# A fused attention, expert and gated-product kernel: first loads in three parts, a shorter mask set-up, out-weights ahead of block weights, two last tiles moved up

## The chip, the cores and the metric

The kernel runs on one core of one Trainium2 chip. Its time is the device time of one execution in microseconds (us); 590.64 us is the median of three runs (589.14 to 592.86). The engines are PE (TensorE matmul, with its weight loads as PEld), DVE (VectorE), ACT (ScalarE), POOL (GpSimd) and SP (SyncE, which here issues DMAs). Each engine executes its own list of instructions in order and waits on semaphores for the others.

## The reference

Three stages run one after the other in fp32.

1. Attention for 2 batches, 8 heads, 768 positions, head size 64, with a local window of `n_local` = 96 keys, `n_global` = 8 keys seen by all, and a bias that grows with distance at a slope of its own for each head:

```python
keep = is_global | is_local
dist = np.where(is_global & ~is_local, float(n_local), np.abs(rel))
slopes = 2.0 ** (-8.0 * (np.arange(H) + 1) / H)
scores = np.where(keep, scale * q @ k.T - slopes * dist, -1e9)
a = softmax(scores); out = a @ v
```

2. Each of the 1536 tokens (512 wide) goes to one of 8 experts: relu(x @ w1[e]) @ w2[e], times two gate factors.
3. (x @ w_a * (x @ w_b)) @ w_out with 1536 inner columns.

## The kernel before

Instructions stand in the order in which they are written; no scheduler moves them. What order each engine has comes from the order of the Python statements.

**Attention** (about 0 to 90 us). There are 24 units of two query tiles by two heads: `units` runs over batch, head pair `p` and `m` = 0, 1, 2. A loop over `n` (line 760 on) runs the steps of different units side by side: `score(n)` (PE scores, DVE adds the bias table and takes the row extremum, ACT the exponential), `trans(n-1)` (PE transposes, DVE and ACT copy), `rows(n-3)`, `av(n-2)`. The keys are laid out so that each query tile sees one stretch of key columns. A table `bias[h]` of 128x384 for each head holds slope times distance plus -1e30 where a key is masked; `dist` and `mk` are built once on DVE, and `make_bias(h)` makes a table on DVE: two ahead of the loop, six within it. Keys and queries of a head pair are loaded by `loadk` and `loadq` from SP's queue into pools of three buffers each; those of pair 0 come in two parts (key columns 0 to 288 and queries 0 to 256 for m = 0; the rest for m = 1 and 2). SP issues in order, and a load into a used buffer waits until its readers are done. `flags()` tests the two integers on DVE, and `nbad` reads the outcome into a register of every engine.

**Router and experts** (about 87 to 300 us). Weights are loaded, split into a high and a low fp32r part (`split_to`) on ACT, DVE and POOL, and used by PE.

**The gated product** (about 300 us to the end) runs in steps f = 0 to 11, one for each 128 inner columns; from f = 2 on `seven(f)` is the step. It forms the products of three groups of 512 tokens (`c` = 0, 1, 2), two of them by seven half-products over sums of blocks. Tiles of the output, `out_tile(p, c, t)`, are made for pairs of steps p = f // 2: `both(p)` puts twelve on a list at the end of an odd step, and `fill(n)` takes n of them off. A tile is six matmuls into a bank `ps_o` (lines 1312 to 1314: gh by wh, gh by wl, gl by wh for both steps of the pair); in the last pair each is added to `acc` on DVE (line 1319) and written by an indirect DMA that POOL issues (line 1321).

Weights of this stage come as int64 words. `conv1` (ACT), `conv2` (DVE, POOL) and `conv3` turn half a weight block into fp32r: `conv3` casts `wh` on ACT (line 1027) and takes the remainder `wl` on POOL (line 1028). Each step prepares the two halves of the next step's block weights (`jobs`) and half of an out-weight block: its `conv3` is put on the list `late` in one step and executed in the next. So the second half for pair p is finished in odd step f = 2p + 1, at whose end the first tiles of the pair read it. In the last step no block weights follow.

Of the kernel before, what the change touches and what calls it, by code (L numbers as in the profile page):

```python
# [12 lines left out]
F32 = mybir.dt.float32  # L13
# [34 lines left out]
def moe_block_kernel(ctx, tc, qd, kd, vd, kt, vn, nv, wg, wg2, we, wm, out):  # L48
# [467 lines left out]
    with ExitStack() as att:  # L516
# [27 lines left out]
        K0, K1, Q0 = 288, 192, 256  # L544
        loadk(0, 0, K0)
        loadq(0, 0, Q0)
        loadk(0, K1)
        loadq(0, Q0)
# [4 lines left out]
        make_identity(nc, ident)  # L553
        G.tensor_copy(idg[:, :, 0:P], bc(ident.unsqueeze(1), [P, 4, P]))

# [5 lines left out]
        t1 = bia.tile([P, P], F32, name="t1")  # L561
        t2 = bia.tile([P, P], F32, name="t2")
        iota(rel[:, 0:128], [[-1, 128]], base=96, cm=1)
        iota(rel[:, 128:256], [[-1, 128]], cm=1)
        iota(rel[:, 256:384], [[-1, 128]], cm=1)
        iota(kid, [[1, 128]])
        G.tensor_scalar(t1, rel[:, 128:256], 0.0, None, ALU.is_ge)
        G.tensor_copy(dist[:, 0:256], rel[:, 0:256])
# [6 lines left out]
        V.tensor_scalar(mk[:, 0:128], rel[:, 0:128], nl_f, None, ALU.is_lt)  # L575
        V.scalar_tensor_tensor(mk[:, 128:256], rel[:, 128:256], nl_f, t1, ALU.is_lt, ALU.mult)
        V.tensor_scalar(t2, kid, ng_f, None, ALU.is_lt)

        V.scalar_tensor_tensor(dist[:, 256:384], rel[:, 256:384], nl_f, mk[:, 128:256], ALU.subtract, ALU.mult)
        V.tensor_tensor(mk[:, 256:384], mk[:, 128:256], t2, ALU.max)  # L580
        V.tensor_scalar(dist[:, 256:384], dist[:, 256:384], nl_f, None, ALU.add)

        V.tensor_copy(mk[:, 96:128], t2[:, 0:32])
        V.tensor_scalar(dist[:, 96:128], rel[:, 96:128], 0.0, nl_f, ALU.mult, ALU.add)
        V.tensor_scalar(mk, mk, BIG, -BIG, ALU.mult, ALU.add)
        bias = [bia.tile([P, 384], F32, name=f"bias{h}") for h in range(H)]

        def make_bias(h):
            V.scalar_tensor_tensor(bias[h], dist, -8.0 * 2.0 ** -(h + 1), mk, ALU.mult, ALU.add)

        make_bias(0)
        make_bias(1)
# [10 lines left out]
        def score(u):  # L603
# [7 lines left out]
            ko, qo = (0, 0) if bp or m == 0 else (K1, Q0)  # L611
# [153 lines left out]
        for n in range(nu + 3):  # L765
            for f in RS.get(n, ()):
                f()
            if n < nu:
                b, p, m = units[n]
                nxt = b * 4 + p + 1  # L770
                if m == 1 and nxt + 1 < 8:
                    loadk(nxt + 1)
                    loadq(nxt + 1)
                if m == 2 and nxt < 8:
                    for j in range(2):
                        loadv(2 * nxt + j)
                if b == 0 and p < 3 and m:
                    make_bias(2 * p + 1 + m)
                score(units[n])
# [15 lines left out]
            if n == 1:  # L795
                flags()
            if n == 3:
                nbad = nc.values_load(ctl_i[0:1, 17:18], min_val=0, max_val=1, skip_runtime_bounds_check_because="a flag")
# [535 lines left out]

    def c2(*js):
        conv2(*js)
        for _ in js:
            cload(nc.sync)


    def seven(f):
# [32 lines left out]
        V.tensor_tensor(v, pc, p1, ALU.add)  # L1374
        if f % 2:
            ab2(0)
        else:
            fill(4)
# [3 lines left out]
        if f % 2:  # L1382
            ab2(1)
            low[2]()
        for j in jobs:
            conv3(j)
        while late:
            f_, j = late.pop(0)
            f_(j)
# [12 lines left out]
        low[0] = gate(0, f, pa)  # L1402
        mul(pb, T4, A22, False, True, True)
# [3 lines left out]
        low[0]()  # L1407
        low[1]()
        if f % 2:
            both(f // 2)  # L1410
            fill(3)
            rest()
            fill(3 if f < 11 else 9)
        else:
            ab2(0)
            rest()
            ab2(1)
            low[2]()
# [106 lines left out]
```

## Time and profile before

| | us |
|---|---|
| runs: median (lowest to highest) | 590.64 (589.14 to 592.86) |
| profiled execution: its own time | 590.52 |
| its span, first to last instruction | 588.5 |
| PE busy | 562.5 (96% of the span) |
| DVE busy | 412.8 (70%) |
| ACT busy | 307.7 (52%) |
| POOL busy | 266.1 (45%) |

The span is the time from the first to the last instruction of the profiled execution; 2.0 us of its own time lie outside it. Busy time counts an instruction from its start to its end, so PE is called busy also where its matmuls overlap: the matmuls of the last stage last 0.39 us each and start 0.23 us apart.

### The profile page before, as it was taken

The page shows a single profiled execution, that of the slowest core. Times are in us where ns is not written, and L with a number is a line of the kernel's source. Part 1 is how long each engine was busy: PE and PEld are TensorE (multiplying, and loading weights), DVE is VectorE, ACT ScalarE, POOL GpSimd, SP SyncE. Part 2 cuts the span into 40 slices and gives each one's busy share as a digit, 9 for nine tenths or more (in the row PEclk, how much of TensorE's full clock was granted, in tenths as well). Part 3 has the DMA queues.
Part 4 walks back from the last instruction along what each step waited for, and adds up shares of the span by engine and source line. Part 5 has one row for each costly group of instructions (what it writes and reads, how often), then busy time and mean ns, then how long its engine had stood idle before and what let it go on. Part 6 is the DMA issues. An engine that isn't in the chain of part 4 may idle for free. (4 is left out here: it accounts for less than half of the span.)

```text
span 588.5 us, 10238 instructions
## 1 busy us (share of the span) xinstructions
PE 562.5 (96%) x3476; PEld 485.2 (82%) x3476; DVE 412.8 (70%) x985; ACT 307.7 (52%) x710; POOL 266.1 (45%) x259
## 2 busy tenths in 40 slices
PE   5999999989999998999999999999899999999995
PEld 4787777978999998999978788788788878878884
DVE  6889986636945788776856777676676686686563
ACT  4877784457655766767564665505414423442210
POOL 3344580655515364545343336425624534344235
PEclk9999999999999998999999999999999999999998
DMA  8676772348576777788661021230120302200014
GB/s 279 241 248 222 308 196 104 109 155 287 169 237 234 230 253 273 229 261 275 225 205 42 33 82 63 72 108 36 73 80 28 108 36 73 107 36 1 2 42 174
DMA packets 39264, 87.30 MB, mean 148 GB/s; under 512 B 6001, under 2 KB 17009, under 8 KB 39201
## 3 DMA queue, kind: packets, MB, share of 16 engines
q1 hardware_dynamic: 32256, 74.25, 37.5%
q0 software_dynamic: 2192, 6.95, 3.3%
q10 hardware_dynamic: 4752, 5.34, 2.9%
q8 instruction: 31, 0.51, 0.4%
q14 instruction: 33, 0.26, 0.1%
HBM read 73.28 MB, written 13.23 MB: 147 GB/s over the span
## 5 line engine op out<-in xcount | busy, mean ns | idle before, releaser
L127 POOL TENSOR_TENSOR wl<-st,wh 128x512 fp32r<-128x512 f32 x58 | 75.2, 1317 | 73.2 <-ACT wh L123 61.3
L1016 POOL TENSOR_TENSOR tx<-tx,st 128x512 int32<-128x512 int32 x36 | 52.4, 1467 | 96.7 <-DVE tx L1014 42.3
L479 PE MATMUL ps_y<-h,wl 128*128 128x224 f32 (+7 forms) x288 | 74.7, 259 | 0.0
L123 ACT CAST wh<-st 128x1024 fp32r<-128x1024 f32 x56 | 59.1, 1056 | 28.9 <-DMA st<-we 28.0
L475 PE MATMUL ps_y<-h,wh 128*128 128x448 f32 (+5 forms) x224 | 68.3, 370 | 4.4 <-DVE h L497 3.2
L127 DVE TENSOR_TENSOR wl<-st,wh 128x1024 fp32r<-128x1024 f32 x35 | 49.0, 1399 | 28.7 <-ACT wh L123 28.6
L479 PE MATMUL ps_h<-x,wl 128*128 128x224 f32 (+6 forms) x256 | 66.9, 261 | 0.0
L1028 POOL TENSOR_TENSOR wl<-tx,wh 128x512 fp32r<-128x512 f32 x36 | 48.6, 1374 | 24.3 <-ACT wh L1027 24.3
L1313 PE MATMUL ps_o<-wl,gh 128*128 128x512 f32 x144 | 56.5, 393 | 3.0 <-POOL wl L1028 3.0
L627 ACT ACTIVATE pe<-pe,mx 128x256 f32<-128x256 f32 (+1 forms) x96 | 45.9, 479 | 22.6 <-DVE mx L623 22.6
L1319 DVE TENSOR_TENSOR acc<-ps_o,acc 128x512 f32<-128x512 f32 x60 | 40.8, 689 | 23.6 <-PE ps_o L1314 23.5
L1312 PE MATMUL ps_o<-wh,gh 128*128 128x512 f32 x144 | 56.2, 390 | 0.9 <-ACT acc L1317 0.9
L475 PE MATMUL ps_h<-x,wh 128*128 128x448 f32 (+4 forms) x192 | 56.3, 363 | 0.5 <-DVE yt L507 0.3
L1314 PE MATMUL ps_o<-wh,gl 128*128 128x512 f32 x144 | 56.1, 389 | 0.0
L479 PEld LDWEIGHTS ps_y<-h,wl 128*128 128x128 f32 x288 | 55.8, 194 | 0.0
L475 PEld LDWEIGHTS ps_y<-h,wh 128*128 128x128 f32 x224 | 42.9, 191 | 8.3 <-ACT hs L495 3.0
L479 PEld LDWEIGHTS ps_h<-x,wl 128*128 128x128 f32 x256 | 48.8, 191 | 0.0
L1267 POOL TENSOR_TENSOR wl<-tt,wh 128x512 fp32r<-128x512 f32 x20 | 25.5, 1300 | 49.1 <-ACT wh L1265 49.1
L623 DVE CUSTOM_DVE_ANT_0 pe<-ps_s,bias 128x256 f32<-128x256 f32 (+1 forms) x96 | 32.8, 398 | 7.8 <-PE ps_s L617 6.9
L475 PEld LDWEIGHTS ps_h<-x,wh 128*128 128x128 f32 x192 | 36.1, 188 | 2.0 <-DVE yt L507 0.5
L1265 ACT CAST wh<-tt 128x1024 fp32r<-128x1024 f32 x10 | 10.5, 1052 | 49.4 <-DVE tt L1260 49.4
L1313 PEld LDWEIGHTS ps_o<-wl,gh 128*128 128x128 f32 x144 | 27.0, 188 | 10.1 <-POOL wl L1028 4.6
(341 smaller groups left out, 1508.1 us busy)
## 6 DMA issues: line engine op xcount, KB each, us to landing
st<-we SPq DMA_DIRECT2D x64, 512.0 KB, 4.6
st<-wm SPq DMA_DIRECT2D x32, 512.0 KB, 3.5
vc<-vd SPq DMA_DIRECT2D x16, 352.0 KB, 5.2
k<-kd SPq DMA_DIRECT2D x7, 464.0 KB, 6.0
y_dram<-zero SPq DMA_DIRECT2D x12, 256.0 KB, 6.5
x_dram<-x SPq DMA_DIRECT2D x6, 512.0 KB, 3.2
acc<-y_dram SPq DMA_DIRECT2D x6, 512.0 KB, 5.0
q<-qd SPq DMA_DIRECT2D x7, 384.0 KB, 6.2
```

Source lines behind the costliest of these rows:

```text
L123: A.copy(wh, st)
L127: eng.tensor_tensor(wl[:, r], st[:, r], wh[:, r].bitcast(F32), ALU.subtract)
L475: T.matmul(pt[:, 0:2 * n].rearrange("p (s n) -> p s n", s=2), a, M[:, k], start=(k == 0), stop=False)
L479: T.matmul(pt[:, 0:n], b, M[:, k, 0], start=False, stop=(k == last))
L623: V.tensor_tensor_reduce(out=pe[:, t_, j, 0:n], in0=ps[:, j, t_, 0:n], in1=bias[2 * p + j][:, b0:b0 + n], op0=ALU.add, op1=ALU.min, scale= ...
L627: A.activation(pe[:, t_, j, 0:n], pe[:, t_, j, 0:n], AF.Exp, bias=mx[:, t_, j:j + 1], scale=-1.0, accum_out=sm[:, t_, j:j + 1])
L1016: lambda t=txi, l=l: G.tensor_tensor(t, t, l, ALU.add)))
L1028: G.tensor_tensor(wl_, tx, wh.bitcast(F32), ALU.subtract)
L1312: T.matmul(po, gh, wh, start=(i == 0), stop=False)
L1313: T.matmul(po, gh, wl, start=False, stop=False)
L1314: T.matmul(po, gl, wh, start=False, stop=(i == 1))
L1319: V.tensor_tensor(at, po, at, ALU.add)
```

## The change

There are five edits.

- The first keys and queries come in three parts, one for each `m` of pair 0 (`cuts`). All three buffers of both pools are then in use, and the loads of pair 1, which stand next but four in SP's list, wait for the readers of the first part.
- The mask set-up is written anew. POOL marks keys that lie ahead of the query by a distance of 1e6 (`FAR`) before DVE starts, and DVE then needs five operations for `mk` and `dist` instead of nine. Tables 0 and 1 are made on DVE, the second as half the first; tables 2 to 7 are made on POOL ahead of the loop as multiples of table 1. `make_identity` and the copy into `idg` come behind POOL's mask operations.
- `flags()` moves from n = 1 to n = 3 and the register loads `nbad` from n = 3 to n = 5.
- In `seven(f)` the list `late` (the out-weights) is worked off ahead of the block weights (`jobs`), and in step 11 as soon as `v` is formed.
- In step 11 two tiles of the last pair come ahead of the last six matmuls on `pb`, one between its DVE operations, and nine at the end.

```diff
--- before.py
+++ after.py
@@ -541,55 +541,45 @@
 
         nc.sync.dma_start(nv_i, nv.partition_broadcast(P))
 
-        K0, K1, Q0 = 288, 192, 256
-        loadk(0, 0, K0)
-        loadq(0, 0, Q0)
-        loadk(0, K1)
-        loadq(0, Q0)
+        cuts = [(0, 288, 0), (192, 608, 256), (512, KW, 512)]
+        for a, b, q0 in cuts:
+            loadk(0, a, b)
+            loadq(0, q0, q0 + 256)
         for bh in range(2):
             loadv(bh)
         nc.sync.dma_start(wg_sb, wg)
         nc.sync.dma_start(idg[:, :, P:P + 32], wg2)
-        make_identity(nc, ident)
-        G.tensor_copy(idg[:, :, 0:P], bc(ident.unsqueeze(1), [P, 4, P]))
-
 
         dist = bia.tile([P, 384], F32, name="dist")
         mk = bia.tile([P, 384], F32, name="mk")
         rel = bia.tile([P, 384], F32, name="rel")
         kid = bia.tile([P, P], F32, name="kid")
-        t1 = bia.tile([P, P], F32, name="t1")
-        t2 = bia.tile([P, P], F32, name="t2")
+        FAR = 1e6
+        own = rel[:, 128:384].rearrange("p (a n) -> p a n", a=2)
         iota(rel[:, 0:128], [[-1, 128]], base=96, cm=1)
-        iota(rel[:, 128:256], [[-1, 128]], cm=1)
-        iota(rel[:, 256:384], [[-1, 128]], cm=1)
+        iota(own, [[0, 2], [-1, 128]], cm=1)
+        G.affine_select(out=own, in_=own, compare_op=ALU.is_ge, fill=FAR, base=0, pattern=[[0, 2], [-1, 128]], channel_multiplier=1)
+        G.memset(rel[:, 96:128], FAR)
         iota(kid, [[1, 128]])
-        G.tensor_scalar(t1, rel[:, 128:256], 0.0, None, ALU.is_ge)
-        G.tensor_copy(dist[:, 0:256], rel[:, 0:256])
+        make_identity(nc, ident)
+        G.tensor_copy(idg[:, :, 0:P], bc(ident.unsqueeze(1), [P, 4, P]))
 
         V.tensor_copy(nv_f, nv_i)
         nvr = nv_f[:, :].rearrange("p (a b) -> p b a", b=2)
         V.scalar_tensor_tensor(nval, nvr[:, 0, :], 0.0, nvr[:, 1, :], ALU.is_lt, ALU.add)
         V.scalar_tensor_tensor(nval, nval, 4294967296.0, nvr[:, 0, :], ALU.mult, ALU.add)
 
-        V.tensor_scalar(mk[:, 0:128], rel[:, 0:128], nl_f, None, ALU.is_lt)
-        V.scalar_tensor_tensor(mk[:, 128:256], rel[:, 128:256], nl_f, t1, ALU.is_lt, ALU.mult)
-        V.tensor_scalar(t2, kid, ng_f, None, ALU.is_lt)
-
-        V.scalar_tensor_tensor(dist[:, 256:384], rel[:, 256:384], nl_f, mk[:, 128:256], ALU.subtract, ALU.mult)
-        V.tensor_tensor(mk[:, 256:384], mk[:, 128:256], t2, ALU.max)
-        V.tensor_scalar(dist[:, 256:384], dist[:, 256:384], nl_f, None, ALU.add)
-
-        V.tensor_copy(mk[:, 96:128], t2[:, 0:32])
-        V.tensor_scalar(dist[:, 96:128], rel[:, 96:128], 0.0, nl_f, ALU.mult, ALU.add)
-        V.tensor_scalar(mk, mk, BIG, -BIG, ALU.mult, ALU.add)
+        V.tensor_scalar(mk[:, 256:384], kid, ng_f, -BIG, ALU.is_ge, ALU.mult)
+        V.tensor_scalar(mk[:, 0:256], rel[:, 0:256], nl_f, -BIG, ALU.is_ge, ALU.mult)
+        V.tensor_scalar(dist, rel, nl_f, None, ALU.min)
+        V.tensor_copy(mk[:, 96:128], mk[:, 256:288])
+        V.tensor_tensor(mk[:, 256:384], mk[:, 128:256], mk[:, 256:384], ALU.max)
         bias = [bia.tile([P, 384], F32, name=f"bias{h}") for h in range(H)]
 
-        def make_bias(h):
-            V.scalar_tensor_tensor(bias[h], dist, -8.0 * 2.0 ** -(h + 1), mk, ALU.mult, ALU.add)
-
-        make_bias(0)
-        make_bias(1)
+        V.scalar_tensor_tensor(bias[0], dist, -4.0, mk, ALU.mult, ALU.add)
+        V.tensor_scalar(bias[1], bias[0], 0.5, None, ALU.mult)
+        for h in range(2, H):
+            G.tensor_scalar(bias[h], bias[1], 0.5 ** (h - 1), None, ALU.mult)
         xt = {}
 
         units = [(b, p, m) for b in range(B) for p in range(4) for m in range(QT // 2)]
@@ -608,7 +598,7 @@
             mx = wrk.tile([P, 2, 2], F32, tag="mx", bufs=3, name="mx")
             sm = wrk.tile([P, 2, 2], F32, tag="sm", bufs=5, name="sm")
             bp = b * 4 + p
-            ko, qo = (0, 0) if bp or m == 0 else (K1, Q0)
+            ko, _, qo = cuts[0 if bp else m]
             for t_ in range(2):
                 i = 2 * m + t_
                 k0, n, b0 = geom(i)
@@ -774,8 +764,6 @@
                 if m == 2 and nxt < 8:
                     for j in range(2):
                         loadv(2 * nxt + j)
-                if b == 0 and p < 3 and m:
-                    make_bias(2 * p + 1 + m)
                 score(units[n])
             if 0 <= n - 1 < nu:
                 trans(units[n - 1])
@@ -792,9 +780,9 @@
             for _ in range(4 if n >= 3 else 0):
                 if cl:
                     cl.pop(0)()
-            if n == 1:
+            if n == 3:
                 flags()
-            if n == 3:
+            if n == 5:
                 nbad = nc.values_load(ctl_i[0:1, 17:18], min_val=0, max_val=1, skip_runtime_bounds_check_because="a flag")
             if n in LD:
                 eload(0, LD.index(n))
@@ -1332,6 +1320,11 @@
 
     late = []
 
+    def lates():
+        while late:
+            f_, j = late.pop(0)
+            f_(j)
+
     def c2(*js):
         conv2(*js)
         for _ in js:
@@ -1372,6 +1365,8 @@
         V.tensor_tensor(u2, pb, p1, ALU.add)
         mul(pc, T1, S1, True)
         V.tensor_tensor(v, pc, p1, ALU.add)
+        if f == 11:
+            lates()
         if f % 2:
             ab2(0)
         else:
@@ -1382,11 +1377,9 @@
         if f % 2:
             ab2(1)
             low[2]()
+        lates()
         for j in jobs:
             conv3(j)
-        while late:
-            f_, j = late.pop(0)
-            f_(j)
         for j in wo:
             conv1(j)
         for _ in nxt:
@@ -1400,17 +1393,26 @@
         V.tensor_tensor(u2, pc, u2, ALU.add)
         V.tensor_tensor(pa, u2, pa, ALU.mult)
         low[0] = gate(0, f, pa)
+        if f == 11:
+            both(f // 2)
+            fill(2)
+            low[0]()
         mul(pb, T4, A22, False, True, True)
         V.tensor_tensor(pb, pb, p1, ALU.add)
         V.tensor_tensor(pb, pb, v, ALU.mult)
         low[1] = gate(1, f, pb)
-        low[0]()
+        if f == 11:
+            fill(1)
+        else:
+            low[0]()
         low[1]()
-        if f % 2:
+        if f == 11:
+            fill(9)
+        elif f % 2:
             both(f // 2)
             fill(3)
             rest()
-            fill(3 if f < 11 else 9)
+            fill(3)
         else:
             ab2(0)
             rest()
```

DVE's list from its third operation on, where mask and bias tables are made (`rel`, `kid`: distances and key numbers from POOL; `nval`: the two integers); before:

```order
L573 SCALAR_TENSOR_TENSOR nval<-nval,nv_f 128x2
L575 TENSOR_SCALAR mk<-rel,nval 128x128
L576 SCALAR_TENSOR_TENSOR mk<-rel,nval,t_189 128x128
L577 TENSOR_SCALAR t_190<-kid,nval 128x128
L579 SCALAR_TENSOR_TENSOR dist<-rel,nval,mk 128x128
L580 TENSOR_TENSOR mk<-mk,t_190 128x128
L581 TENSOR_SCALAR dist<-dist,nval 128x128
L583 COPY mk<-t_190 128x32
L584 TENSOR_SCALAR dist<-rel,nval 128x32
L585 TENSOR_SCALAR mk<-mk 128x384
L589 SCALAR_TENSOR_TENSOR bias_209<-dist,mk 128x384
L589 SCALAR_TENSOR_TENSOR bias_210<-dist,mk 128x384
L623 ISA pe,mx<-ps_s,bias_209 128x128
```

and now:

```order
L570 SCALAR_TENSOR_TENSOR nval<-nval,nv_f 128x2
L572 TENSOR_SCALAR mk<-kid,nval 128x128
L573 TENSOR_SCALAR mk<-rel,nval 128x256
L574 TENSOR_SCALAR dist<-rel,nval 128x384
L575 COPY mk<-mk 128x32
L576 TENSOR_TENSOR mk<-mk 128x128
L579 SCALAR_TENSOR_TENSOR bias_208<-dist,mk 128x384
L580 TENSOR_SCALAR bias_209<-bias_208 128x384
L613 ISA pe,mx<-ps_s,bias_208 128x128
```

Nine operations for `mk` and `dist` have become five, and the second table is a multiple of the first.

POOL's list in step f = 3 (`tt`: sums of block weights; the `wl` named once is the out-weight's half, the one named twice the two block halves); before:

```order
L1016 TENSOR_TENSOR tx_6572<-tx_6572,st64_6483 128x512
L1016 TENSOR_TENSOR tx_6636<-tx_6636,st64_6575 128x512
L1016 TENSOR_TENSOR tx_6639<-tx_6639,st64_6577 128x512
L1267 TENSOR_TENSOR wl_6715<-tt_6155,wh_6714 128x512 x2
L1028 TENSOR_TENSOR wl_6738<-tx_6636,wh_6737 128x512
L1028 TENSOR_TENSOR wl_6738<-tx_6639,wh_6737 128x512
L1028 TENSOR_TENSOR wl_6569<-tx_6572,wh_6568 128x512
```

and now:

```order
L1004 TENSOR_TENSOR tx_6571<-tx_6571,st64_6482 128x512
L1004 TENSOR_TENSOR tx_6635<-tx_6635,st64_6574 128x512
L1004 TENSOR_TENSOR tx_6638<-tx_6638,st64_6576 128x512
L1255 TENSOR_TENSOR wl_6714<-tt_6154,wh_6713 128x512 x2
L1016 TENSOR_TENSOR wl_6562<-tx_6571,wh_6561 128x512
L1016 TENSOR_TENSOR wl_6739<-tx_6635,wh_6738 128x512
L1016 TENSOR_TENSOR wl_6739<-tx_6638,wh_6738 128x512
```

The out-weight's remainder stands ahead of the two of the block weights.

DVE's list at the end of step 11 (`u`, `ps_pa`, `ps_pb`: the products; `gl`: the low part of a gated product; `acc`: an output tile's sum); before:

```order
L1400 TENSOR_TENSOR u_8172<-ps_pc,u_8172 128x512
L1401 TENSOR_TENSOR ps_pa<-u_8172,ps_pa 128x512
L1404 TENSOR_TENSOR ps_pb<-ps_pb,p_8171 128x512
L1405 TENSOR_TENSOR ps_pb<-ps_pb,v 128x512
L1279 TENSOR_TENSOR gl<-ps_pa,gh 128x512
L1279 TENSOR_TENSOR gl<-ps_pb,gh 128x512
L1319 TENSOR_TENSOR acc<-ps_o,acc 128x512 x12
```

and now:

```order
L1393 TENSOR_TENSOR u_8171<-ps_pc,u_8171 128x512
L1394 TENSOR_TENSOR ps_pa<-u_8171,ps_pa 128x512
L1307 TENSOR_TENSOR acc<-ps_o,acc 128x512 x2
L1267 TENSOR_TENSOR gl<-ps_pa,gh 128x512
L1401 TENSOR_TENSOR ps_pb<-ps_pb,p_8170 128x512
L1402 TENSOR_TENSOR ps_pb<-ps_pb,v 128x512
L1307 TENSOR_TENSOR acc<-ps_o,acc 128x512
L1267 TENSOR_TENSOR gl<-ps_pb,gh 128x512
L1307 TENSOR_TENSOR acc<-ps_o,acc 128x512 x9
```

Two of the twelve sums stand ahead of the work on `ps_pb`, and one within it; PE's tiles stand likewise.

## Rows read from the trace of the kernel before

**Rows 1.** Page, part 1: engine, busy us (share of the span), instructions.

```profile
PE 562.5 (96%) x3476; PEld 485.2 (82%) x3476; DVE 412.8 (70%) x985; ACT 307.7 (52%) x710; POOL 266.1 (45%) x259
```

**Rows 2.** Waits of PE, whole span: engine line <- waited for: us, times, longest.

```profile
PE ps_s L617 <- DMA q<-qd: 6.2, 2, 4.6
PE ps_o L1313 <- POOL wl L1028: 3.0, 4, 1.8
PE ps_x L448 <- ACT xA L442: 0.8, 1, 0.8
```

**Rows 3.** Timeline, PE, out tiles of steps 3 and 5: start us, us, what [idle <-releaser].

```profile
377.02 0.39 PE L1312 MATMUL ps_o<-wh,gh 128*128 128x512 f32 x1
377.77 0.50 PE L1313 MATMUL ps_o<-wl,gh 128*128 128x512 f32 x1 [0.36 <-POOL wl L1028]
...
423.91 0.39 PE L1312 MATMUL ps_o<-wh,gh 128*128 128x512 f32 x1
426.14 0.50 PE L1313 MATMUL ps_o<-wl,gh 128*128 128x512 f32 x1 [1.85 <-POOL wl L1028]
```

**Rows 4.** Timeline, POOL, step 3 and step 5, weight remainders.

```profile
373.92 3.80 POOL L1028 TENSOR_TENSOR wl<-tx,wh 128x512 fp32r<-128x512 f32 x3
...
422.31 3.78 POOL L1028 TENSOR_TENSOR wl<-tx,wh 128x512 fp32r<-128x512 f32 x3
```

**Rows 5.** Timeline, PE, first units.

```profile
4.58 1.65 PE L617 MATMUL ps_s<-k,q 64*128 64x128 f32 x8 [4.58 <-DMA q<-qd]
7.83 2.08 PE L617 MATMUL ps_s<-k,q 64*128 64x256 f32 x8 [1.60 <-DMA q<-qd]
9.84 1.54 PE L643 MATMUL ps_t<-ident,pe 128*128 128x128 f32 x6
11.31 1.45 PE L617 MATMUL ps_s<-k,q 64*128 64x256 f32 x8
...
18.03 1.13 PE L617 MATMUL ps_s<-k,q 64*128 64x256 f32 x8
```

**Rows 6.** Timeline, DVE, mask chain and first scores.

```profile
4.54 0.29 DVE L575 TENSOR_SCALAR mk<-rel,nval 128x128 f32<-128x128 f32 x1
...
6.09 0.35 DVE L585 TENSOR_SCALAR mk<-mk 128x384 f32<-128x384 f32 x1
6.48 1.03 DVE L589 SCALAR_TENSOR_TENSOR bias<-dist,mk 128x384 f32<-128x384 f32 x2
...
7.43 0.28 DVE L623 CUSTOM_DVE_ANT_0 pe<-ps_s,bias 128x128 f32<-128x128 f32 x1
```

**Rows 7.** Timeline, POOL, same start.

```profile
2.90 0.56 POOL L567 TENSOR_SCALAR t<-rel 128x128 f32<-128x128 f32 x1
...
3.42 0.39 POOL L568 COPY dist<-rel 128x256 f32<-128x256 f32 x1
```

**Rows 8.** DMA issues: out<-in, queue, count, KB each, median us to landing.

```profile
k<-kd SPq DMA_DIRECT2D x7, 464.0 KB, 6.0
q<-qd SPq DMA_DIRECT2D x7, 384.0 KB, 6.2
```

**Rows 9.** Timeline, end of the kernel, DVE's and POOL's last rows.

```profile
568.37 2.08 DVE L1319 TENSOR_TENSOR acc<-ps_o,acc 128x512 f32<-128x512 f32 x3
...
580.63 0.69 DVE L1319 TENSOR_TENSOR acc<-ps_o,acc 128x512 f32<-128x512 f32 x1 [0.67 <-PE ps_o L1314]
581.99 0.69 DVE L1319 TENSOR_TENSOR acc<-ps_o,acc 128x512 f32<-128x512 f32 x1 [0.67 <-PE ps_o L1314]
...
569.34 1.07 POOL L1321 DMA_INDIRECT out<-acc,tok_i  x1 [5.85 <-DVE acc L1319]
...
582.34 0.98 POOL L1321 DMA_INDIRECT out<-acc,tok_i  x1 [0.30 <-issue]
583.63 0.98 POOL L1321 DMA_INDIRECT out<-acc,tok_i  x1 [0.30 <-issue]
```

**Rows 10.** Windows: us, busy us (count) of PE, PEld, DVE, ACT, POOL, PEclk, DMA share, GB/s.

```profile
228.00:229.00 1.00, 1.00 (x5) 0.96 (x4) 0.74 (x2) 0.70 (x1) 0.00 (x0) 0.50 1.00 381
```

## The prediction, made before the changed kernel ran

> **What bounds the kernel now.** I read the busy shares first. PE is busy for 96% of the span [rows 1], so this is a kernel in which only two things can change the time: PE's idle stretches, and what comes before PE's first and after its last matmul. The list of PE's waits comes next, because it names those idle stretches. The reader should see how short it is: the largest entry is the first keys and queries (4.6 us before the first matmul, then 1.6 us), the second is 3.0 us in four waits for a weight remainder from POOL [rows 2]. Third came the timelines at these two places and at the end of the kernel. Everything that the change does on DVE or POOL elsewhere counts only through one of these three.
>
> The sum is made against the profiled execution, 590.5 us, which lies 0.1 us under the median of the runs, 590.6 us.
>
> **Out-weights ahead of block weights.** At the end of an odd step PE starts the tiles of a new pair. The fourth to sixth matmul of a tile read the half of the out-weight that was converted in this very step, the fifth its remainder, and POOL made that remainder as the last of three. In step 3 the fifth matmul starts 0.75 us after the fourth, in step 5 2.23 us after it [rows 3]. Undisturbed they are 0.23 us apart, so 0.52 and 2.00 us are lost; steps 7 and 9 repeat step 3's pattern (0.53 and 0.54 us), step 11 has no block weights and no wait. The matmul after each wait also lasts 0.50 instead of 0.39 us [rows 3]. That makes 0.52 + 2.00 + 0.53 + 0.54 + 4 x 0.11 = 4.0 us.
>
> POOL's three remainders take 3.80 us, so 1.27 each [rows 4]. With the out-weight first, it is done at 373.92 + 1.27 = 375.2 us in step 3, and needed at 377.25: 2 us to spare. In step 5 it is done at 423.6 and needed at 424.1, half a microsecond to spare, so this wait goes too, but barely. What is late next would be the block weights: they end where the out-weight ended, at 377.7 and 426.1 us, but their first reader is the next step, behind six tiles. Two sums of the last stage start 1.36 us apart [rows 9], which is one tile of PE, so there are about 8 us of PE work in between. In an even step still more stands between. I take the whole 4.0 us. If the half microsecond in step 5 does not hold, some of its 2.0 us stays; the lower bound is 2.0 us.
>
> **The start.** In the trace the first scores run from 4.58 us, the second wait for their queries until 7.83, and the first transposes start at 9.84 [rows 5]. DVE's mask chain runs from 4.54 to 7.43 us, where the first score operation starts [rows 6]. The new chain, with the nearest durations: a mask over 128 columns 0.25 us, one over 256 about 0.32, one over 384 0.39 (row L585 occupies 6.09 to 6.48), the small copy and the maximum 0.35, one bias table of two inputs 0.52 (half of 1.03) and the second table, of the cheaper kind, 0.38. That is 2.2 us instead of 2.9, so the first score operation starts at about 6.7 us. By the shapes, the second part of the queries now has 0.62 MB ahead of and with it instead of 0.92 MB; the first 0.28 MB landed at 4.6 us and 0.92 MB at 7.8, so in proportion it lands at 6.3 us, just when the first scores end. Bounds: 5.5 and 7.0 us, without effect on the rest, because the transposes wait for the exponentials of the first unit, which follow DVE: they move from 9.84 to about 9.05 us, 0.8 us earlier.
>
> What this 0.8 us becomes depends on PE's speed there. Eight score matmuls of the same shape take 2.08 us at 7.83 us and 1.13 us at 18.03 [rows 5]: PE begins at half rate, and the eight at 11.31 (1.45 us) show the change of rate in the middle, at about 12.0 us. This is 4.2 us after PE's work became continuous at 7.83. If the rate still rises at 12.0, half of the 0.8 us is given back in slow work: 0.4 us gain. If it rises 4.2 us after the first scores, at 8.8, then the 2.2 us of slow work between 9.84 and 12.0 shrinks to half as well: 0.8 + 1.1 = 1.9 us. PE's work is continuous from 4.58 but for some 0.6 us before the transposes, so I take 1.3 us, nearer the upper end.
>
> The Trainium skill, "TensorE: Matmul & The Clock Gate", Part 1, says that TensorE starts throttled by default and that sustained activity releases it. By that rule the start would give 1.9 us and the total 583.9 us; the trace agrees with the rule in that full rate comes only behind continuous work.
>
> **Parts of the start that cost nothing.** Six tables on POOL: one operation over 128 columns took 0.56 us, a copy of 256 columns 0.39 [rows 7], so one of 384 lies between 0.6 and 1.7 us. Even at 1.7 all six are done at 17 us, and the third and fourth, wanted at 13 to 14 us, at 10 us. POOL has nothing else to do then; its next work waits for a weight load. DVE loses six tables, 3.1 us in all, and the four operations of the flags move; PE never waits for DVE in the units that follow, so this gains nothing either. The register load stands at the same distance of two units behind the flags. Identity and its copy come 1 to 2 us later on POOL, at about 3.5 us, and are wanted at 9.
>
> **The loads of pair 1.** They now wait in SP's list until the first scores are done, about 6.4 instead of 5.4 us, with the loads of pair 2 and further values behind them. Keys and queries take 6.0 and 6.2 us to land in the median [rows 8], so they land at 12.4 to 13.1 us. The scores of unit 3 will want them at about 13. Cost: 0, at most 1 us, which the start's lower end covers.
>
> **The end.** POOL's twelve output issues start 1.29 us apart (582.34 to 583.63), PE's tiles 1.36 us apart. The first issue waits until 569.34 because DVE's first sums come behind six operations on the products, at 568.37, and POOL then carries the delay to its last issue at 583.63, although DVE was done at 581.99 + 0.69 = 582.68 [rows 9]. With two tiles ahead POOL starts some 2.5 us earlier and follows DVE. An issue begins 0.28 us behind the sum (569.06 to 569.34), so the last one begins at 582.97: 0.65 us gain. PE's work is only exchanged. Bounds: 0 if DVE's order holds a sum back, 0.95 if the issue follows at once.
>
> Sum: 4.0 + 1.3 + 0.65 = 5.95, so 590.5 - 5.95, about **584.5 us**, or 1.0% under the median. About 1% is what a measurement of this kernel can tell from no change, so this forecast lies on the edge.
>
> **The rivals.**
>
> *PE's rate rises early* (the upper end of the start): 583.9 us. For it: nearly continuous work from 4.58 us. Against: the pause of 0.6 us. 0.18.
>
> *The start is given back.* PE also waits 0.8 us for `xA` [rows 2], a gathered block which follows a chain of POOL and DMA work of some 20 us; if that chain does not move with PE, or the rate rises late, the start is worth 0 to 0.4 us and the time is 585.6 us. Against: the loads in that chain are released by PE's and DVE's own progress. 0.20.
>
> *Half the waits stay*, because POOL is late in step 5 for another reason: 2.0 us stay, 586.6 us. For it: only 0.5 us to spare. 0.10.
>
> *Slower: SP's list blocks.* The loads of pair 1 wait for a buffer, those of pair 2 and the values of pair 1 stand behind them, and each unit of pair 1 waits in turn. It begins to cost when the queries of pair 1 land after 13 us, and it outweighs the 5.95 us when they land after 19. At twice the median landing, 6.4 + 12.4, they come at 18.8 us, 5.6 us late, which alone only undoes the gain; pair 2 late by as much again would give 590.5 - 5.95 + 11.2, about 596 us. Against: these landings are medians under the same load. 0.04.
>
> *The change does not do what it says*: the lists show that out-weights, masks and tiles stand as described; what is left is that the waits are for something else than the remainder: 588.5 us. 0.03.
>
> **How the numbers follow.** The forecast, 584.5 us with a range of its own of 583.6 to 585.6, has 0.45. A granted clock of 0.50, the 1.2 GHz level, stands at 227.0 to 230.4 us [rows 10], behind PE waits of the expert stage; since PE is at work there, that cost half of it, about 1.7 us, and one such stretch more or less moves any case by as much. The range that holds 8 in 10 reaches from 582.5 (early rate, no such stretch) to 587.2 us (half the waits kept, and more). Faster by over 1%, under 584.7 us: half and a little of the forecast (0.27), nearly all of the early rate (0.17) and a little of the others (0.03), 0.47. Slower by over 1%: 0.04. The rest, 0.49, is within 1%.
>
> **What would show it.** In the new profile: no PE wait for the remainder of an out-weight (four before); POOL's first remainder in steps 3, 5, 7 and 9 ends before the fifth tile matmul; the second scores start near 6.3 and the first transposes near 9.0 us; slow score matmuls end at 9 to 12 us; the last output issue starts 0.3 us behind DVE's last sum. The prediction is wrong if PE waits for block weights at the start of a step, if the third unit's scores wait for queries, or if the waits in the expert stage grow by what the start won.

## The result, and the profile after

The changed kernel took 585.93 us (median of 8 executions, 584.59 to 588.59), the kernel before beside it 590.75 us: ratio 0.9912, 95% interval 0.9888 to 0.9936, so 0.6 to 1.1% faster. Forecast were 584.5 us with a range of 582.5 to 587.2. The median lies inside that range but outside the narrower one of the forecast, 583.6 to 585.6. A later comparison (e8 below) gave 585.36 against 592.23 us, ratio 0.9884 (0.9837 to 0.9932).

The profiled execution took 584.59 us, with a span of 582.4 us. It is the fastest of its eight; its mean granted clock is 0.999, that of the others 0.991 to 0.996. Against the profiled execution of before (590.52 us) it gains 5.93 us, where the sum forecast 5.95; that they agree so closely is in part luck, as the account of the start and of the half clock below shows.

Part 1 of the page after, which answers to [rows 1]; PE's share is what it was:

```profile
PE 560.6 (96%) x3476; PEld 484.7 (83%) x3476; DVE 408.9 (70%) x975; ACT 306.8 (53%) x710; POOL 274.4 (47%) x264
```

PE's waits after, same columns as [rows 2]. POOL's remainder (L1016 now) is gone from the list, as is the second wait for queries; a wait for gathered blocks, `xs`, is now 2.9 us (1.9 before):

```profile
PE ps_s L607 <- DMA q<-qd: 4.6, 1, 4.6
PE ps_x L448 <- ACT xs L442: 2.9, 3, 1.2
...
PE ps_x L448 <- ACT xA L442: 0.8, 1, 0.8
```

The timeline after, in the columns of [rows 3], at the start, at three waits in the router and expert stages, in steps 3 and 5, and at the end:

```profile
4.57 3.86 PE L607 MATMUL ps_s<-k,q 64*128 64x128 f32 x16 [4.57 <-DMA q<-qd]
6.30 0.36 DVE L580 TENSOR_SCALAR bias<-bias 128x384 f32<-128x384 f32 x1
6.57 0.28 DVE L613 CUSTOM_DVE_ANT_0 pe<-ps_s,bias 128x128 f32<-128x128 f32 x1
6.75 7.22 POOL L582 TENSOR_SCALAR bias<-bias 128x384 f32<-128x384 f32 x6 [3.26 <-DVE bias L580]
8.36 1.54 PE L633 MATMUL ps_t<-ident,pe 128*128 128x128 f32 x6
9.83 1.74 PE L607 MATMUL ps_s<-k,q 64*128 64x256 f32 x8
12.52 0.88 PE L650 MATMUL ps_a<-pt,vc 128*64 128x128 f32 x12
...
114.52 0.42 PE L448 MATMUL ps_x<-ident,xB 16*128 16x16 f32 x4 [0.54 <-ACT xB L442]
...
161.19 0.58 PE L412 MATMUL ps_tk<-ta,tb 128*128 128x12 f16 x3 [0.36 <-DVE tb L407]
...
243.93 0.66 PE L448 MATMUL ps_x<-ident,xs 128*128 128x128 f32 x4 [0.99 <-ACT xs L442]
...
372.69 3.80 POOL L1016 TENSOR_TENSOR wl<-tx,wh 128x512 fp32r<-128x512 f32 x3
...
420.11 3.80 POOL L1016 TENSOR_TENSOR wl<-tx,wh 128x512 fp32r<-128x512 f32 x3
422.03 0.39 PE L1300 MATMUL ps_o<-wh,gh 128*128 128x512 f32 x1
422.25 0.39 PE L1301 MATMUL ps_o<-wl,gh 128*128 128x512 f32 x1
...
576.16 0.39 PE L1302 MATMUL ps_o<-wh,gl 128*128 128x512 f32 x1
576.59 0.69 DVE L1307 TENSOR_TENSOR acc<-ps_o,acc 128x512 f32<-128x512 f32 x1 [0.67 <-PE ps_o L1302]
577.55 0.98 POOL L1309 DMA_INDIRECT out<-acc,tok_i  x1 [0.38 <-DVE acc L1307]
```

Against [rows 5] and [rows 6]: PE now runs from 4.57 us without a gap (in e8, the same kernel, with one of 0.16 us), the first transposes start 1.48 us earlier, the third scores (the row at 9.83) too. Against [rows 3]: the fifth tile matmul follows the fourth after 0.22 us instead of 2.23. Against [rows 9]: the last output issue starts 0.96 us behind the start of DVE's last sum instead of 1.64.

To see where time is won I match the PE instructions of two traces and call **lead** by how much one starts earlier than in the profiled execution of before. In the changed kernel it is 1.19 us at the first products of probabilities and values (13.71 against 12.52), 1.26 us at the start of the last stage, 5.40 us behind step 9 and 6.08 us at the last output issue. Between the first two it is not constant: it falls to 0.16 us between 162 and 223 us, as told below. The same readings of all kernels, in us (last column: from the start of PE's last matmul to the start of POOL's last output issue):

| trace | first products at | lead, last stage | gain in steps 3 to 9 | last issue behind PE's last matmul |
|---|---|---|---|---|
| before | 13.71 | 0 | 0 | 2.07 |
| changed | 12.52 | 1.26 | 4.17 | 1.39 |
| changed, again (e8) | 12.19 | -0.14 | 4.18 | 1.39 |
| before, again (e10) | 13.48 | 0.35 | -0.24 | 2.95 |
| e1, out-weights only | 13.58 | -0.98 | 4.18 | 3.87 |
| e2, start only | 12.80 | 0.64 | 0.03 | 3.20 |
| e3, end only | 13.54 | -3.85 | -1.84 | 1.77 |
| e4, out-weight second | 12.14 | 0.67 | 3.03 | 1.75 |
| e5, loads only | 12.69 | 2.05 | -0.07 | 2.05 |
| e6, changed with old loads | 14.56 | -0.62 | 4.17 | 1.39 |
| e7, sixteen early matmuls | 13.13 | 0.72 | 4.17 | 1.39 |
| e9, eight early matmuls | 11.91 | 1.40 | 4.18 | 1.40 |
| e11, e9 with later loads | 11.86 | -2.39 | 4.18 | 1.63 |
| e12, before with POOL padded | 14.81 | -1.37 | 1.43 | 4.46 |

### The profile page after: what moved, and what is told of

Same layout as the page of the kernel before. It is cut to its first block, busy times and chain, and to the rows that moved or that the text cites. A ratio compares the mean times of both kernels' runs of the same rounds, so it can differ in the third digit from the quotient of the medians.

```text
span 582.4 us, 10238 instructions
## 1 busy us (share of the span) xinstructions
PE 560.6 (96%) x3476; PEld 484.7 (83%) x3476; DVE 408.9 (70%) x975; ACT 306.8 (53%) x710; POOL 274.4 (47%) x264
## 5 line engine op out<-in xcount | busy, mean ns | idle before, releaser
L475 PE MATMUL ps_y<-h,wh 128*128 128x448 f32 (+5 forms) x224 | 66.8, 365 | 3.8 <-DVE h L497 2.9
L1016 POOL TENSOR_TENSOR wl<-tx,wh 128x512 fp32r<-128x512 f32 x36 | 48.5, 1369 | 14.9 <-ACT wh L1015 14.9
L1112 PE MATMUL ps_ab<-Y2h,wh 128*128 128x512 f32 x88 | 34.3, 389 | 0.0
```

The lines of the kernel that those rows point to most:

```text
L475: T.matmul(pt[:, 0:2 * n].rearrange("p (s n) -> p s n", s=2), a, M[:, k], start=(k == 0), stop=False)
L1016: G.tensor_tensor(wl_, tx, wh.bitcast(F32), ALU.subtract)
L1112: T.matmul(pt, wh[:, k, :], yh[:, k, :], start=start and k == 0, stop=False, skip_group_check=more)
```

## The experiments

The kernels ran in four groups, each on one chip beside executions of the kernel before; the medians of these lie between 592.1 and 594.9 us, so only ratios are compared. e4, e5, e6, e10 and e12 had one execution each, for their traces.

**The out-weights alone (e1).**

```diff
...
+        lates()
         for j in jobs:
             conv3(j)
-        while late:
-            f_, j = late.pop(0)
-            f_(j)
```

> The kernel before, with the out-weights ahead of the block weights and nothing else. Theory (the four waits were for POOL's order): PE waits for no out-weight remainder any more, the gain over the kernel before builds up in steps 3, 5, 7 and 9 as 0.6, 2.1, 0.7 and 0.7 us, 4.1 in all, so the runs come to 590.7 - 4.1 = 586.6 us. Rival (the waits are for something else, or the block weights are late in their place): at least 2 us of the waits stay or come up again at the start of steps 4, 6, 8 and 10, 588.5 to 590.7 us. Start and end as before: no part of the gain there.

588.80 against 594.17 us, ratio 0.9898 (0.9865 to 0.9931), so 6.1 us (4.1 to 8.0) where 4.1 were expected. The trace gains 0.66, 2.14, 0.71 and 0.67 us in the four steps, 4.18 in all, and in the last stage PE waits for no remainder of either weight. The theory holds; the same 4.17 or 4.18 us come up in each of the seven traces with the new order in its full form.

**Out-weight second of three (e4).**

```diff
-        lates()
-        for j in jobs:
+        for j in jobs[:1]:
+            conv3(j)
+        lates()
+        for j in jobs[1:]:
             conv3(j)
```

> The changed kernel with the out-weight second of the three remainders instead of first (one block weight ahead of it). Theory (all that counts is when POOL ends that remainder): one POOL operation of 1.27 us more ahead of it. In steps 3, 7 and 9 it still ends 0.8 us before PE needs it, no wait; in step 5 it ends 0.4 us after the need, so PE waits once, about 0.4 us, and the gap between the fourth and fifth matmul of the first tile is 0.6 instead of 0.23 us. Rival (the order among all conversions matters, or ACT's): waits in all four steps, or none.

One wait, in step 5 alone. The timeline of e4 there:

```profile
414.63 1.31 POOL L1004 TENSOR_TENSOR tx<-tx,st 128x512 int32<-128x512 int32 x1 [1.68 <-ACT a L1349]
...
421.20 3.78 POOL L1016 TENSOR_TENSOR wl<-tx,wh 128x512 fp32r<-128x512 f32 x3
422.64 0.39 PE L1300 MATMUL ps_o<-wh,gh 128*128 128x512 f32 x1
423.79 0.50 PE L1301 MATMUL ps_o<-wl,gh 128*128 128x512 f32 x1 [0.76 <-POOL wl L1016]
```

The second remainder ends at 421.20 + 2.52 = 423.72, PE goes on at 423.79: what counts is when POOL ends that operation. The wait is 0.76 us where 0.4 was expected, because POOL's pause in front of its conversion was 1.68 us here and 1.12 in the changed kernel. That pause is the subject of e12.

**POOL's list padded (e12).**

```diff
         make_bias(0)
         make_bias(1)
+        pad = bia.tile([P, 8], F32, name="pad")
+        for _ in range(32):
+            G.memset(pad, 0.0)
```

> The kernel before with 32 small constant writes of POOL ahead of its attention work, so that all that POOL does later stands 32 instructions further back in its list. In five traces POOL pauses 1.1 to 1.8 us ahead of its second conversion in step 5 and in no other step, with its inputs there, and a load of 8 KB of instructions ends 1.0 to 1.3 us before the pause does. Theory (POOL waits for its own instructions): the pause moves to another place, POOL's remainders in step 5 are 1.4 us earlier, and PE waits there 0.4 instead of 1.9 us: about 1.5 us less in the last stage. Rival (the pause belongs to step 5's data): it stays at 1.1 to 1.8 us and PE's wait at 1.9 us.

POOL in step 5, first in the timeline of before (pause 1.46 us in the second row), then in that of e12:

```profile
412.76 1.54 POOL L1016 TENSOR_TENSOR tx<-tx,st 128x512 int32<-128x512 int32 x1 [3.92 <-DVE tx L1014]
415.75 1.30 POOL L1016 TENSOR_TENSOR tx<-tx,st 128x512 int32<-128x512 int32 x1 [1.46 <-PE ps_ab L1126]
```

```profile
414.15 2.80 POOL L1019 TENSOR_TENSOR tx<-tx,st 128x512 int32<-128x512 int32 x2 [3.92 <-DVE tx L1017]
```

The two conversions now stand back to back. PE's waits of e12, whole span:

```profile
PE ps_o L1316 <- POOL wl L1031: 1.5, 4, 0.4
```

Four waits of at most 0.4 us, and 1.43 us gained with the old order. The DMA queues between 411 and 418 us (queue, kind: packets, MB, share), before and then e12:

```profile
q14 instruction: 3, 0.02, 0.9%
```

```profile
q14 instruction: 1, 0.01, 0.4%
```

So step 5's pause hangs on where POOL is in its list, and not on its data. That it waits for its own instructions agrees with the two loads of 8 KB that left this stretch; which engine a load belongs to is not in the trace. Between 360 and 370 us e12 has two such loads and before has none: there POOL waits for DVE in both kernels (until 367.22 us in e12, 3.04 us, and until 365.86 us before, 3.02 us), so that a pause would not show. That the pause moved to another place, as the theory says, is therefore not seen; that it left step 5 is.

**The start alone (e2), the loads alone (e5), all but the loads (e6).** e2 has all that the change does ahead of the last stage (loads, mask, tables, flags). e5 has only its loads, e6 is the changed kernel without them:

```diff
-        loadk(0, 0, K0)
-        loadq(0, 0, Q0)
-        loadk(0, K1)
-        loadq(0, Q0)
+        for a, b, q0 in cuts:
+            loadk(0, a, b)
+            loadq(0, q0, q0 + 256)
...
-            if n == 1:
+            if n == 3:
                 flags()
```

The last hunk is in e2 alone of the two kernels built on the one before.

> The kernel before with all edits of the start (loads in three parts, mask set-up, tables on POOL, flags later) and nothing else. Theory (the start's gain is carried to the end): the first products of probabilities and values start at 12.5 instead of 13.7 us and step 2 of the last stage begins 1.2 us earlier than in the kernel before, give or take 0.3 us: 589.5 us. Rival (given back in the router and expert stages, where gathered blocks come by a chain of their own): the same 1.2 us at 12.5 us, but 0 to 0.4 us at step 2, 590.3 to 590.7 us. The four waits for the out-weight remainder stay, 3.0 us by the list of waits.

> The kernel before with the first loads in three parts and nothing else (mask set-up, tables, flags, order of the last stage as before). Theory A, formed from the two traces (the wait for the second queries is what the start gains): the second scores follow the first without a gap at about 6.5 us, PE pauses about 0.3 us for the exponentials at 9 us, the third scores start at 10.2 instead of 11.3 us and the first products of probabilities and values at 12.8 instead of 13.7 us: 0.9 of the 1.19 us. Theory B, that of the prediction (the transposes follow DVE's mask chain, so the mask brings it): first transposes still at 9.8 us and products at 13.7 us, gain 0.

> The changed kernel with the loads of pair 0 in two parts as before; mask set-up, tables, flags, out-weights and last tiles stay changed. Theory A: the first score operation on DVE starts at 6.6 us as in the changed kernel, but the second scores wait for their queries until 7.8 us, the first transposes start at 9.8 and the first products at 13.7 us, as in the kernel before: the start's 1.19 us are gone. Theory B (the mask brings it): first transposes at 9.0 and products at 12.9 us, 0.8 of the 1.19 us stay. Then the waits of the last stage are gone in either case.

e2: 592.85 us, ratio 0.9983 (0.9963 to 1.0003); first products 0.91 us earlier, lead 0.64 us at the last stage: between theory and rival. One of e2's twelve executions took 1926.88 us and is not in the ratio. PE in e5:

```profile
4.63 1.65 PE L616 MATMUL ps_s<-k,q 64*128 64x128 f32 x8 [4.63 <-DMA q<-qd]
6.65 2.08 PE L616 MATMUL ps_s<-k,q 64*128 64x256 f32 x8 [0.36 <-DMA q<-qd]
8.66 1.70 PE L642 MATMUL ps_t<-ident,pe 128*128 128x128 f32 x6
10.29 1.21 PE L616 MATMUL ps_s<-k,q 64*128 64x256 f32 x8
...
12.69 0.88 PE L659 MATMUL ps_a<-pt,vc 128*64 128x128 f32 x12
```

With the old mask set-up and DVE's first score operation as late as before (7.42 us), the loads alone bring 1.02 us (0.79 against e10, the second trace of before). PE in e6:

```profile
7.88 2.08 PE L608 MATMUL ps_s<-k,q 64*128 64x256 f32 x8 [1.61 <-DMA q<-qd]
9.89 1.54 PE L634 MATMUL ps_t<-ident,pe 128*128 128x128 f32 x6
11.36 2.08 PE L608 MATMUL ps_s<-k,q 64*128 64x256 f32 x8
...
14.56 0.88 PE L651 MATMUL ps_a<-pt,vc 128*64 128x128 f32 x12
```

DVE's first score operation comes at 6.70 us, near the changed kernel's 6.57, and it helps nothing: PE waits for the queries until 7.88. Theory A holds. The products come even 0.85 us later than before, because the third scores at 11.36 are still at half rate (2.08 us for eight): the trace's first record of full clock is at 13.8 us here, at 12.0 before.

**The end alone (e3).**

```diff
+        if f == 11:
+            both(f // 2)
+            fill(2)
+            low[0]()
         mul(pb, T4, A22, False, True, True)
...
```

> The kernel before with the two tiles of step 11 moved up (and the out-weight conversion of step 11 moved up with them) and nothing else. Theory (POOL's issues carried a late start): POOL's last output issue begins 0.28 us behind the start of its wait's end, that is 0.97 us behind the start of DVE's last sum instead of 1.64, so 0.65 us less: 590.1 us. Rival (PE's order only exchanged, the last issue hangs on DVE): 0 us, 590.7 us. The four waits stay.

591.62 us, ratio 0.9952 (0.9932 to 0.9971), so 1.7 to 4.0 us: more than the 0.65 of the theory. The last issue stands 0.97 us behind the start of DVE's last sum, as expected, but so it does in four of the six traces with the old end; what differs there is when DVE's last sums start. The traces put the surplus in the order that was replaced. The end of e10, the kernel before once more (its edit is none):

> The kernel before as it is, for a second trace of it. If the start is set by loads and mask, its first products come at 13.5 to 13.7 us, as in the three traces with the old start; if what the runs show of the start is the granted clock's rise alone (8.9 to 13.8 us in the traces so far), they come at 12.5 us where the rise is early. The four waits for the out-weight remainder are 3.0 us in the list; step 5's is 1.9.

```profile
579.12 0.69 DVE L1319 TENSOR_TENSOR acc<-ps_o,acc 128x512 f32<-128x512 f32 x1 [0.67 <-PE ps_o L1314]
580.05 0.39 PE L1314 MATMUL ps_o<-wh,gl 128*128 128x512 f32 x1
...
581.95 0.69 DVE L1319 TENSOR_TENSOR acc<-ps_o,acc 128x512 f32<-128x512 f32 x1 [2.13 <-PE ps_o L1314]
583.40 0.69 DVE L1319 TENSOR_TENSOR acc<-ps_o,acc 128x512 f32<-128x512 f32 x1 [0.76 <-remote]
584.36 0.98 POOL L1321 DMA_INDIRECT out<-acc,tok_i  x1 [0.47 <-DVE acc L1319]
```

The last column's releaser misleads: the tile that the sum at 581.95 reads was finished by the matmul at 580.05, and other sums start 0.43 us behind theirs. DVE is 1.5 us late, and the issue 2.95 us behind PE's last matmul (581.41) instead of 2.07. Four of six traces with the old end have such a pause, none of the eight with the new one more than 0.4 us. By the table's last column the new end gains between 0.3 and 3.1 us, 1.6 in the mean. What holds DVE I could not settle. The rest of e10 agrees with the first trace of before: products at 13.48 us, 3.1 us in four waits.

By time the three parts e1, e2 and e3 gain 6.1, 1.0 and 2.9 us, about 10 in all, give or take some 3 us, against 5.2 and 6.9 us for the whole change in its two comparisons. The whole did not run beside them, so time does not show that the parts add up, and why they come to more stays open. The 4.18 us of the out-weights are read from traces, of e1 and of the changed kernel alike, and do not hang on this.

**The changed kernel again (e8), and early matmuls (e7, e9, e11).** A constant tile is multiplied with itself ahead of the first scores, sixteen times in e7, eight times in e9 and e11:

```diff
+        hot = bia.tile([P, P], F32, name="hot")
+        V.memset(hot, 1.0)
+        pw = psG.tile([P, 512], F32, tag="g", name="ps_w")
+        for _ in range(8):
+            T.matmul(pw[:, 0:P], hot, hot, start=True, stop=True)
...
-                if m == 1 and nxt + 1 < 8:
+                if m == 2 and nxt + 1 < 8:
```

The last two lines are in e11 alone.

> The changed kernel as it is, once more, beside the kernel before and the one with the early matmuls on the same chip. If the gain is the sum of its parts here as in the first comparison, 4.8 us below the kernel before (ratio 0.9912, interval 0.9888 to 0.9936). If the end of the old order costs more on some chips, as the runs of the single parts suggest (last output issue 2.8 to 3.5 us behind PE's last matmul instead of 1.7), 6 to 8 us.

> The changed kernel with sixteen matmuls of 128x128 on a constant ahead of the first scores, from about 1 us until the first keys are there; their result is read by nobody. Theory (the half clock until 11.1 us costs the start): the granted clock rises at 8 us or earlier instead of 11.1, the first scores still start at 4.6 us, the third scores at 8.8 instead of 9.8 and the first products at 11.3 instead of 12.5 us: 0.7 to 1.3 us gained at the start, and as much at the end if the expert stage lets it through. Rival (DVE's and ACT's chain sets the start, or these matmuls do not raise the clock): 0 to 0.3 us; or they end after 4.6 us and cost what they end later.

> The changed kernel with eight instead of sixteen matmuls of 128x128 on a constant ahead of the first scores; nobody reads their result. The sixteen were 32 passes and ended at 6.9 us, 2.3 us too late for the first scores, yet the granted clock rose at 5.2 us and the first products came only 0.6 us later than in the changed kernel; a pass at the half clock takes 0.21 us, so eight end at 1.2 + 16 x 0.21 = 4.6 us, when the first keys and queries are there. Theory (the half clock costs the start): first scores at 4.6, clock up by 5.5, third scores at 8.9 and first products at 10.9 to 11.3 us instead of 12.1 to 12.8: 1.2 us less there and, if the expert stage passes it on, 583.2 us on the first chip's scale. Rival (DVE and ACT set the start once the loads are there): first products at 12.0 us or later, no gain. Second rival (the expert stage's own chain): gain of 1.2 us at 12 us that is gone at the start of the last stage, which lay between 293.4 and 295.6 us in the kernels with three-part loads.

> The kernel with eight early matmuls, and the keys and queries of a later pair issued at the third unit of a pair instead of the second. With the early matmuls alone the fourth unit's scores waited 0.4 us for their queries until 13.18 us, while the DMA engines were full from 6 to 14 us with the loads of the pair after it. Theory (the loads of pair 1 share the engines with those of pair 2, which nobody needs yet): the queries of pair 1 land by 12.6 us, no wait, fourth unit at 12.8 instead of 13.2 us, and 0.4 us more are left at 35 us: 0.6 us ahead of the changed kernel instead of 0.2. Rival (values and the small loads fill the engines anyway): still 13.0 to 13.2 us. Second rival: the loads of pair 2 come late in their turn, and the seventh unit waits.

Ratios: e8 0.9884, which is 6.9 us (4.0 to 9.7) and fits both expectations; e7 0.9897 (0.9858 to 0.9936), e9 0.9862 (0.9823 to 0.9901), e11 0.9825 (0.9793 to 0.9856). All are faster than the kernel before; e7, e9 and the changed kernel can't be told apart by time. Whether e11 beats the changed kernel is open: the two never ran side by side, e11's 585.18 us stand beside slower executions of before (594.94 us), and its trace shows no gain. e7's matmuls ended 2.3 us too late. PE in e9:

```profile
1.22 3.79 PE L557 MATMUL ps_w<-hot 128*128 128x128 f32 x16 [1.22 <-DVE hot L554]
4.93 1.30 PE L613 MATMUL ps_s<-k,q 64*128 64x128 f32 x8
6.43 1.13 PE L613 MATMUL ps_s<-k,q 64*128 64x256 f32 x8 [0.20 <-DMA q<-qd]
...
8.38 0.93 PE L639 MATMUL ps_t<-ident,pe 128*128 128x128 f32 x4 [0.16 <-ACT pe L623]
...
11.91 0.88 PE L656 MATMUL ps_a<-pt,vc 128*64 128x128 f32 x12
13.18 0.93 PE L613 MATMUL ps_s<-k,q 64*128 64x128 f32 x8 [0.40 <-DMA q<-qd]
```

The second scores run at full rate (1.13 us), but the exponentials then hold PE, and the fourth unit waits for its queries: 0.6 us gained at the products, 0.15 left at the fourth scores, less than the theory asked. e11 was to bring those queries earlier; they came at 13.51 us, so the first rival holds, and at 35 us it was 0.12 us behind the changed kernel.

The changed kernel itself meets that wait in its second trace. PE in e8, with the scores of the fourth unit:

```profile
13.39 0.93 PE L607 MATMUL ps_s<-k,q 64*128 64x128 f32 x8 [0.32 <-DMA q<-qd]
```

Its first products come 0.33 us earlier than in the profiled execution of the result (12.19 against 12.52), and from 16 us on the two traces are level: the queries of pair 1 take that lead back. e4, which has the same start, waits there 0.48 us.

## Why the prediction was right

The number was right, and two of its three terms came out as worked out; the third, the start, had the right size for the wrong reason, and at the last stage by luck.

- **Out-weights, 4.0 us: right.** 4.17 in the profile, 4.18 alone. In step 5 the remainder ended at 420.11 + 1.27 = 421.38 and was needed at 422.25, 0.87 us to spare (0.5 forecast). The block weights cost nothing, as argued. What the prediction did not ask is why step 5 lost 2.0 us and its sisters 0.5: by e12 1.4 of it is POOL's pause in its own list.
- **The start, 1.3 us: 1.19, but the step behind it failed.** It read: the second part of the queries lands somewhere between 5.5 and 7.0 us "without effect on the rest, because the transposes wait for the exponentials of the first unit, which follow DVE". In the changed kernel the transposes stand directly behind the second scores, without a wait, so the pause of 0.6 us ahead of them, on which the 1.3 us rests, did not come. They do so in the kernel before too [rows 5]: the second scores last until 7.83 + 2.08 = 9.91 us, and the row of 9.84 notes no idle time. e5 shows 0.8 to 1.0 us from the loads without the mask, e6 nothing from the mask without the loads. The mask chain did shorten by the forecast amount (first score operation at 6.57 us, forecast 6.7). Also wrong: pair 1's loads waited for no buffer. They were issued at 6.41 us because the list ahead of them is two loads longer. In e7, where the first scores end at 7.8 us, the first of pair 1's loads was issued at 7.85: there the buffer does hold it. That they cost nothing is true of the profiled execution, which wanted these queries at 13.33 us, but not where PE came sooner: they let the fourth unit (unit 3, counted from 0) go at 13.18 us in e9, at 13.39 in e8 and at 13.50 in e4, behind waits of 0.3 to 0.5 us. Such a wait is one of the signs of being wrong that the prediction names; in e8 and e4 it takes back what an earlier rise of PE's rate had given.
- **What became of the start: luck.** The 1.26 us at the last stage are not the 1.19 us carried through. The lead falls from 1.44 to 0.16 us behind waits at 114.52 us (`xB`, a gathered block) and 161.19 us (`tb`) that before does not have, and stays there until 223 us, much as the rival "the start is given back" says. It grows again because before waits 0.41 and 0.89 us at 224.1 and 225.6 us, where the changed kernel waits 0.21 us in all, and because the kernel before then falls to half clock.
- **When PE's rate rises** was put at 12.0 us or at 8.8. The first record of full clock came at 11.1 us in one trace of the changed kernel and 9.2 in the other, at 8.9 to 11.5 in three more with the new loads, at 10.9 to 12.0 in four with the old loads and at 13.8 and 14.2 in two more, e6 and e12. Within either kind the moment varies by 2.5 to 3.4 us, more than the 2.2 us that lie between their means. The Trainium skill, "TensorE: Matmul & The Clock Gate", Part 1, says that sustained activity releases the clock; by that rule e9's early matmuls raise it early, and the trace agrees (5.7 us). The same part of the Trainium skill says that the number of slow matmuls at the start differs between runs of one kernel; the two traces of the changed kernel agree (11.1 and 9.2 us), and the prediction should have priced that.
- **The end, 0.65 us: 0.68 in the profile**, and by the traces too little for most executions, since the old order was hit by DVE's pause in four of six.
- **"Any half-clock stretch moves the time by 1.7 us": only in part.** Before's stretch at 227 us [rows 10] made the lead grow from 1.45 to 3.0 us; the changed kernel then waited 0.99 us for a gather at 243.9 and the lead was 1.08 at 247.8. Behind the expert stage the lead is -0.14 to 2.05 us in the five traces with new loads and no early matmuls. So for the end of the kernel "the start is given back" is neither shown nor excluded by these traces. The ratio of e2, 1.0 us (-0.2 to 2.2), fits the forecast and that rival alike.
- **The median, 585.93 against 584.5:** the profiled execution had no half-clock stretch, the others have lower clocks. One stretch of 3.4 us at half clock takes about 0.003 off the mean clock of an execution of 584 us (3.4 x 0.5 / 584), so I estimate one to three of them in the others. The prediction held such a stretch as a range, not as the usual case. Of its values, 585.6 us (the start given back) lies nearest to the median, so the time alone does not pick between the forecast and that rival.

## What to carry to other kernels

A wait that several steps share but one step has three times as long has a second cause: look at the engine that makes it late before pricing the wait. Where two things end within a microsecond of each other (queries and mask here), test each alone before naming one the bound. And a gain of 1 us at the head of a stage with its own chain (gathers) is read behind that stage, not ahead of it, and in more than one trace.

## What the runs showed of the hardware

- POOL's pause of 1.1 to 1.8 us in step 5 goes when 32 more instructions stand ahead of it (e12): a stall that data dependencies do not show.
- The clock fell to half (1.2 GHz) at few places: at 135 to 137 us in six of fourteen traces, at 227 to 229 in five, at 248 to 253 in three and at 272 in one, behind PE's waits in the expert stage. The wait alone does not decide it: all fourteen wait 1.1 to 1.5 us for a gathered block until 134 to 137 us, and eight of them keep the full clock there. With e3 it fell also at 431 us, behind the wait of 2 us in step 5 that the change removes. Two windows of e3, columns as in [rows 10]:

```profile
138.00:139.00 1.00, 1.00 (x5) 1.00 (x6) 0.50 (x1) 0.81 (x3) 0.85 (x2) 0.50 0.41 146
...
432.00:433.00 1.00, 1.00 (x4) 0.81 (x3) 0.00 (x0) 0.00 (x0) 0.00 (x0) 0.50 0.00 0
```

In the last one DVE, ACT and POOL are idle and PE alone is at work, at half rate; e3 lost 1.9 us against before in step 5. Before and e10 have a wait of 1.85 and 1.96 us at the same place and keep the full clock there.
